# A fused attention and mixture-of-experts kernel: the places of the list fill, of some routing steps, of the first loads and of constant matmuls

## The chip, the cores and the metric

The kernel runs on one core of a Trainium2 chip. The metric is the device time of one execution in microseconds (us); less is better. The median of three executions of the kernel before is 837.98 us.

## The reference

Attention over 8 batches and 8 heads, 576 tokens of 64 values, with a mask by blocks of 64; its output, one row of 512 for each of 4608 tokens, goes through a top-1 mixture of 8 experts. Cut to what matters:

```python
scores = (q @ k.T) / 8                       # for each batch and head, 576 x 576
scores = where(i // 64 >= j // 64, scores, -1e9)
attn = exp(scores - max); attn /= sum(attn) + 1e-9
x = (attn @ v) as rows of 8 * 64             # 4608 x 512
logits = x @ w_gate + modality_bias[modality_id]
e = argmax(logits); gate = softmax(logits)[e]
out = gate * (relu(x @ w1[e]) @ w2[e])       # w1: 512 x 1024, w2: 1024 x 512
```

## The kernel before

Work goes by pairs of heads: 32 pairs, four to a batch. A slot is one pass over the table `ORDER`: it runs the scores, maxima and exponentials of pair `slot` and, one stage later, the transposes, value products and back products of pair `slot - 1`. Slot 0 has its own table, `FIRST`, and the last pass another, `LAST`. Every matmul operand is split into a rounded part and a rest (fp32r), so that three products give nearly full precision: `first_keys`, `first_copies` and `first_queries` do this for pair 0 in three pieces (`PIECES`), `second` for pair 1, `split_qk` on GpSimd for the others, one slot ahead.

The order on each engine, and in SyncE's queue of transfers, is the program's own: within an engine everything waits for what stands ahead of it. Names in the tables: S scores, M maxima (VectorE, `low`, L290), E exponentials (ScalarE), T transposes, C and D their copies and rests (ScalarE and VectorE), X, Y, W the three parts of the value product (`values`, L421), x and y its copies, K the back product (L440, L442), Z the rows (L453); the letter A or B is the head of the pair, t the last 64 tokens of both.

`load` issues the loads of a pair; for pairs 0 and 1 also the mask rows `cm`, four partitions of the tile z, which GpSimd issues. `load_q` issues the queries of the pair two slots on. The rests of the last 64 tokens' probabilities go through the transfer `p<-p4l` (L384), issued at the end of a slot and read in the next slot's value product, part W.

`keep_warm` issues matmuls of constants into a bank that nobody reads at that time; `WARM` says how many ahead of which step.

Routing of a batch (`routing`) is a list of about 28 small steps, most of them on VectorE; `steps` holds those still to come. The places q0 to q7 of `ORDER` take one step each, or two in slots 25 to 30 (from `EARLY`); qp and qv take only the matmul step `counts` and the scan behind it. After the last pair of a batch (place ZB) all steps that are left run at once and the next batch's list begins. Behind batch 5's routing, 22 steps of the expert choice follow in the list (`choose`, through `Later`, kind "pick"). Routing works in the upper half of the bank o0, part X of the value product in its lower half, so X waits for the routing steps ahead of it.

The list of token numbers by expert (`idlist`, in device memory) is first filled with a number that is out of bounds, in eight transfers of 304 KB from one small tile (`prepare_fill`); the scatters of each batch (L579) then write into it. Before, the fill's tile is a part of `btmp`, set by GpSimd as one of batch 0's steps, and the eight transfers are steps too, with empty steps between them.

Of the kernel before, what the change touches and what calls it, by code (L numbers as in the profile page):

```python
# [14 lines left out]
I32 = mybir.dt.int32  # L15
# [9 lines left out]
NPAIR = B * H // 2  # L25
# [40 lines left out]
FIRST += tuple(x for x in ORDER if x[1] == 0 and x not in FIRST and x[0][0] != "q")  # L66

PIECES = ((slice(0, 256), slice(0, 256)), (slice(256, 576), slice(256, 640)), (slice(576, 1280), slice(640, 1280)))
WARM = {(0, "SA3"): 14, (0, "SB01"): 14, (0, "TA0"): 5, (0, "St1"): 8, (0, "TA1"): 16, (0, "TA2"): 12, (1, "TB0"): 6}

EARLY_STEPS = {
    (NPAIR - 2, "SA2"): ("stage", "ids", "cast00"),
# [30 lines left out]
def attention_moe(ctx, tc, qk, vr, bkw, w1, w2, cf, ci, cm, ld, out):  # L103
# [24 lines left out]
    midf = cst.tile([128, 2, B * 5], F32, name="midf")  # L128
    bias = cst.tile([128, B * 5, NE], F32, name="bias")
    btmp = cst.tile([128, B * 5, NE], F32, name="btmp")  # L130
    fill = btmp.rearrange("p a b -> p (a b)").bitcast(I32)[:, 0 : NROW // 128]

    att_stack = ExitStack()
    rt = ctx.enter_context(tc.tile_pool(name="rt", bufs=2, side="right"))
# [25 lines left out]
    xrb = [rt.tile([128, 4, XW], F32, name=f"xr{i}", bufs=1) for i in range(2)]  # L160
    for x in xrb:
        dve.memset(x[:, :, 513:XW], 0.0)
    scatters, placing = [], []
    pairs = [Pair() for _ in range(NPAIR)]
    xrs = {}

    def load(p):
        d = pairs[p]
        d.qk = qkts[p % 3]
        d.q = d.qk[:, 0:1280].rearrange("p (h c) -> p h c", h=2)  # L170
        d.k = d.qk[:, 1280:2432].rearrange("p (h c) -> p h c", h=2)
        d.qt = d.qk[:, 2432:2560]
        d.raw = raws[p % 2]
        d.q2, d.k2, d.pt = q2s[p % 2], k2s[p % 2], pts[p % 2]
        d.s, d.pm, d.copies, d.o, d.ot, d.b = {}, {}, {}, {}, {}, {}
        d.ott = None
        d.rq = att.tile([128, 1280], F32, name="pm", bufs=3) if p == 1 else rawq
        if p == 0:
            for ks, qs in PIECES:
                nc.sync.dma_start(d.raw[:, ks], qk[p][:, 1280:2560][:, ks])  # L180
                nc.sync.dma_start(d.rq[:, qs], qk[p][:, qs])
        elif p == 1:
            for h in range(2):
                ks, qs = halves(h)
                nc.sync.dma_start(d.raw[:, ks], qk[p][:, 1280:2560][:, ks])
                nc.sync.dma_start(d.rq[:, qs], qk[p][:, qs])
        else:
            nc.sync.dma_start(d.raw, qk[p][:, 1280:2560])
        if p < 2:
            pool.dma_start(zs[p][64:68], cm)  # L190

    def load_q(p):
# [504 lines left out]
    def prepare_bias(dst, r):  # L697
# [10 lines left out]
        lambda: pool.tensor_tensor(bias, bias, btmp, ALU.add),  # L708
        lambda: dve.tensor_copy(ranks, iom8),
        lambda: dve.tensor_copy(bases, base8),  # L710
        lambda: pool.memset(fill, int(BIG)),
    ]
    for i in range(IW // 2):
        steps += [lambda i=i: prepare_fill(i)] + [lambda: None] * (0 < i < 6)

    def keep_warm(n):
        for _ in range(n):
# [2 lines left out]
    def run_slot(slot):  # L720
# [7 lines left out]
        for name, stage in LAST if slot == NPAIR else ORDER if slot else FIRST:  # L728
# [13 lines left out]
            if name == "q4" and 0 < slot < NPAIR - 1:  # L742
                load_q(slot + 2)
            if name[0] == "q":
                kinds = (name,) if not name[1].isdigit() else ("",) if name in ("q1", "q4") else ("", "pick")
                for _ in range(2 if EARLY * PPB < slot < NPAIR - 1 and "" in kinds else 1):
                    if slot > 1 and steps and getattr(steps[0], "kind", "") in kinds:
                        steps.pop(0)()
                continue
# [3 lines left out]
            if slot == 0:  # L753
                done.add((name, p))
                if name in first:
                    first[name]()
                    continue
            keep_warm(WARM.get((slot, name), 0))
            emit(name, p)
            if name == "vh":  # L760
                for _ in range(2 if slot % PPB == 0 or slot > EARLY * PPB else 1):
# [11 lines left out]
    with tc.manual_schedule(engines=engines | {ET.SP}):  # L773
        load(0)
        for _ in range(NWARM):
            pe.matmul(bbank, ones, jks[0], start=True, stop=True)
        nc.sync.dma_start(cft[:, 0:128], cf[:, 0:128])
        load(1)
        for i in range(2):
            first_keys(i, dve)  # L780
            first_copies(i)
            if i == 0:
                first_queries(0, dve)
        gather_low(pairs[0], (0,))
        for slot in range(NPAIR + lag):
            run_slot(slot)
# [454 lines left out]
```

## Time and profile before

| | us |
|---|---|
| median of three executions (837.08 to 840.86) | 837.98 |
| the profiled execution | 837.02 |
| its span | 835.2 |
| TensorE busy (matmul) | 815.8 |
| VectorE busy | 444.8 |
| ScalarE busy | 463.5 |
| GpSimd busy | 457.0 |

The profile is of one execution. Busy time is the sum over an engine's instructions; matmuls are pipelined and their ends are modelled, so a TensorE that is busy all the time isn't at its peak. What ends a wait is inferred from semaphore events. By the distance of the L442 matmuls a slot takes 11.4 to 11.7 us from slot 1 on (one 13.5), and some 12.2 us in most of slots 26 to 31; the attention stage ends near 390 us, and then the experts' products follow.

### The profile page before, as it was taken

How to read it: one execution, taken by the hardware profiler on the slowest of the kernel's cores; microseconds unless marked ns; L12 is line 12 of the kernel's file. 1: busy time of each engine (PE TensorE's matmuls, PEld its weight loads, DVE VectorE, ACT ScalarE, POOL GpSimd, SP SyncE). 2: the span in 40 equal slices, each digit the busy share in tenths (PEclk: the TensorE clock that was granted, in tenths of full speed). 3: DMA queues.
4: the chain of work that ended last, by engine and by line, in shares of the span. 5: the costliest groups of instructions: out<-in, count | busy, mean ns of one | idle time of the engine just before them, and what ended most of it. 6: DMA issues, size and time to landing. Idle time of an engine off the chain costs nothing.

```text
span 835.2 us, 15342 instructions
## 1 busy us (share of the span) xinstructions
PE 815.8 (98%) x5151; PEld 730.2 (87%) x5151; DVE 444.8 (53%) x1650; ACT 463.5 (55%) x1387; POOL 457.0 (55%) x306
## 2 busy tenths in 40 slices
PE   7999999999999999999999999999999999999995
PEld 6999999999999999999999888888888888888883
DVE  4888999999999999996631112121222212122110
ACT  5989999999999999996432213121221313132221
POOL 6988889898999989987563431222330302010010
PEclk7999999999999999999999999999999999999998
DMA  8678876768786868666723221131230301110000
GB/s 255 195 221 261 245 228 193 240 194 268 199 255 188 241 205 250 191 162 209 252 65 102 78 79 65 34 102 50 77 127 25 127 26 62 56 38 26 26 34 22
DMA packets 59104, 118.46 MB, mean 142 GB/s; under 512 B 13618, under 2 KB 26738, under 8 KB 59016
## 3 DMA queue, kind: packets, MB, share of 16 engines
q1 hardware_dynamic: 49888, 96.30, 38.3%
q0 software_dynamic: 9136, 21.17, 8.0%
q8 instruction: 42, 0.69, 0.4%
q14 instruction: 38, 0.31, 0.1%
HBM read 77.50 MB, written 22.25 MB: 119 GB/s over the span
## 4 chain that ended last, share of the span: by engine, by line
PE 65%; issue 25%; POOL 4%; DMA 2%; DVE 2%; ACT 0%; POOLq 0%; SPq 0%; DVEq 0%
PE o L421 12%; PE s L1016 8%; PE b L440 6%; PE s L285 5%; PE s L286 5%; PE s L960 4%; PE o L1006 4%; PE o L1029 3%; PE t L344 3%; PE t L349 2%; PE s L277 2%; POOL out L1040 2%; PE b L1029 2%; PE s L1029 2%; POOL xr L917 2%
## 5 line engine op out<-in xcount | busy, mean ns | idle before, releaser
L381 DVE TENSOR_TENSOR ptl<-t,pth 128x512 fp32r<-128x512 f32 (+3 forms) x288 | 140.0, 504 | 17.9 <-ACT pth L374 15.8
L290 DVE TENSOR_SCALAR_CACHE_REDUCE scratch<-s 128x128 bf16<-128x128 f32 (+4 forms) x288 | 132.4, 477 | 13.1 <-PE s L286 10.4
L318 ACT ACTIVATE pm<-s,nm 128x256 f32<-128x256 f32 (+3 forms) x256 | 134.6, 535 | 5.7 <-DVE scratch L290 5.5
L374 ACT CAST pth<-t 128x512 fp32r<-128x512 f32 (+3 forms) x288 | 122.9, 453 | 16.2 <-PE t L344 10.9
L421 PE MATMUL o<-pth,vhl 128*128 128x320 f32 (+3 forms) x384 | 110.2, 306 | 2.0 <-DVE pi L577 0.7
L421 PE MATMUL o<-ptl,vhl 128*128 128x320 f32 (+3 forms) x384 | 110.2, 307 | 0.0
L1040 POOL DMA_INDIRECT out<-scratch,ids_b x17 | 16.8, 986 | 165.4 <-ACT scratch L1039 152.3
L285 PE MATMUL s<-qkt 128*128 128x256 f32 (+3 forms) x256 | 90.4, 366 | 1.4 <-DVE qkt L237 1.3
L214 POOL TENSOR_TENSOR qkt<-rawq,qkt 64x1280 fp32r<-64x1280 f32 x30 | 87.7, 2924 | 2.4
L210 POOL TENSOR_TENSOR z<-raw,qkt 64x1152 fp32r<-64x1152 f32 x30 | 79.7, 2655 | 13.3 <-issue 8.5
L286 PE MATMUL s<-z 68*128 68x256 f32 (+3 forms) x256 | 81.0, 329 | 1.0 <-DMA z<-cm 1.0
L421 PEld LDWEIGHTS o<-pth,vhl 128*128 128x128 f32 x384 | 72.7, 189 | 4.9 <-issue 1.8
L1018 ACT ACTIVATE qkt<-s 128x512 fp32r<-128x512 f32 x28 | 16.7, 598 | 103.9 <-PE s L1016 103.9
L1018 ACT ACTIVATE ptl<-s 128x512 fp32r<-128x512 f32 x28 | 16.8, 598 | 103.0 <-PE s L1016 103.0
L421 PEld LDWEIGHTS o<-ptl,vhl 128*128 128x128 f32 x384 | 72.7, 189 | 1.3
L440 PE MATMUL b<-bk,ot 128*128 128x72 f32 x512 | 64.7, 269 | 0.1
L440 PEld LDWEIGHTS b<-bk,ot 128*128 128x128 f32 x512 | 64.2, 192 | 0.6 <-ACT ott L433 0.6
L318 ACT ACTIVATION_READ_ACCUMULATOR pm<-s,nm 128x1 f32 x256 | 53.3, 208 | 0.0
L285 PEld LDWEIGHTS s<-qkt 128*128 128x128 f32 x256 | 49.7, 194 | 2.4 <-DVE qkt L237 1.8
L286 PEld LDWEIGHTS s<-z 68*128 68x128 f32 x256 | 49.7, 194 | 1.5 <-issue 1.3
L1016 PE MATMUL s<-z,w0hb 128*128 128x512 f32 x128 | 50.6, 395 | 0.0
L1016 PE MATMUL s<-z,w0lb 128*128 128x512 f32 x128 | 50.5, 395 | 0.0
(355 smaller groups left out, 2101.7 us busy)
## 6 DMA issues: line engine op xcount, KB each, us to landing
raw<-qk SPq DMA_DIRECT2D x30, 640.0 KB, 4.2
rawq<-qk SPq DMA_DIRECT2D x30, 640.0 KB, 5.1
raw<-w SPq DMA_DIRECT2D x23, 512.0 KB, 3.5
vrt<-vr SPq DMA_DIRECT2D x32, 320.0 KB, 5.2
k2t<-z SPq DMA_DIRECT2D x64, 144.0 KB, 5.3
xrows<-xr SPq DMA_DIRECT2D x8, 1056.0 KB, 6.6
z<-qkt SPq DMA_DIRECT2D x30, 256.0 KB, 4.8
idlist<-btmp SPq DMA_DIRECT2D x8, 304.0 KB, 6.0
```

What stands on the lines that cost most here:

```text
L210: pool.tensor_tensor(d.k2[0:64], k, d.k[0:64], ALU.subtract)
L214: pool.tensor_tensor(d.q[0:64], q, d.q[0:64], ALU.subtract)
L285: pe.matmul(o, d.q[:, h, qs], d.k[:, h, 0:n], start=True, stop=False)
L286: pe.matmul(o, d.q2[0:68, h, qs], d.k2[0:68, h, 0:n], start=False, stop=True)
L290: dve.tensor_scalar(jks[jturn[0] % 4][:, 0 : s.shape[-1]], s, -SCALE, start, ALU.mult, ALU.min, accum_out=o)
L318: act.activation(d.pm[h][:, CHUNK_OFF[c] : CHUNK_OFF[c] + n], s[:, 256 * i : 256 * i + n], AF.Exp, bias=d.nm[:, h, c : c + 1], scale=SCALE ...
L374: act.copy(dst[0], s)
L381: dve.tensor_tensor(dst[1], s, dst[0], ALU.subtract)
L421: pe.matmul(o, w, r, start=part != "W" and i == 0, stop=part != "Y" and i == len(mm) - 1)
L440: pe.matmul(d.b[h][:, 72 * c : 72 * c + 72], d.ot[h][:, 128 * c : 128 * c + 128], w, start=True, stop=True)
L1016: nc.tensor.matmul(hp, w[:, kc, :], x[kc], start=i == 0, stop=i == len(mm) - 1)
L1029: nc.tensor.matmul(y, x[:, ts], w, start=m == 0 and j == 0, stop=m == 7 and j == 2)
```

## The change

- The fill's source is no longer in `btmp` but in the second row buffer `xrb[1]`; GpSimd sets it once, after the loads of pairs 0 and 1 are issued. The eight fill transfers are no longer steps: two go out in each of slots 1 to 4, ahead of Mt1 and of Ttl.
- In slots 25 to 30 the place q2 takes only steps of the kind "pick", up to two; the other numbered places take up to two, as before.
- Pair 0's queries are issued in ScalarE's queue, its keys as before in SyncE's.
- Pair 0's mask rows come in three transfers, the first with what the first two chunks of head 0 need.
- `WARM`: 40 in place of 14 constant matmuls ahead of the scores SA3 of slot 0, 24 in place of 14 ahead of SB01.

```diff
-WARM = {(0, "SA3"): 14, (0, "SB01"): 14, (0, "TA0"): 5, (0, "St1"): 8, (0, "TA1"): 16, (0, "TA2"): 12, (1, "TB0"): 6}
+WARM = {(0, "SA3"): 40, (0, "SB01"): 24, (0, "TA0"): 5, (0, "St1"): 8, (0, "TA1"): 16, (0, "TA2"): 12, (1, "TB0"): 6}
+
+FILLING = ("Mt1", "Ttl")
...
-    fill = btmp.rearrange("p a b -> p (a b)").bitcast(I32)[:, 0 : NROW // 128]
...
+    fill = xrb[1][:, 0, 0 : NROW // 128].bitcast(I32)
...
-                nc.sync.dma_start(d.rq[:, qs], qk[p][:, qs])
+                act.dma_start(d.rq[:, qs], qk[p][:, qs])
...
-        if p < 2:
+        if p == 0:
+            z, m = (t[:, 0:2048].rearrange("p (a c) -> p a c", a=2) for t in (zs[p][64:68], cm))
+            for cs in (slice(0, 256), slice(256, 1024)):
+                pool.dma_start(z[:, :, cs], m[:, :, cs])
+            pool.dma_start(zs[p][64:68, 2048:2176], cm[:, 2048:2176])
+        elif p == 1:
             pool.dma_start(zs[p][64:68], cm)
...
-        lambda: pool.memset(fill, int(BIG)),
     ]
-    for i in range(IW // 2):
-        steps += [lambda i=i: prepare_fill(i)] + [lambda: None] * (0 < i < 6)
...
-                kinds = (name,) if not name[1].isdigit() else ("",) if name in ("q1", "q4") else ("", "pick")
-                for _ in range(2 if EARLY * PPB < slot < NPAIR - 1 and "" in kinds else 1):
+                fast = EARLY * PPB < slot < NPAIR - 1
+                kinds = (name,) if not name[1].isdigit() else ("",) if name in ("q1", "q4") else ("pick",) if fast and name == "q2" else ("", "pick")
+                for _ in range(2 if fast and name[1].isdigit() else 1):
...
             keep_warm(WARM.get((slot, name), 0))
+            if name in FILLING and 0 < slot <= IW // 4:
+                prepare_fill(2 * slot - 2 + FILLING.index(name))
             emit(name, p)
...
         load(1)
+        pool.memset(fill, int(BIG))
```

What moves is shown at three places. SyncE's queue before, from the key gathers of slot 3 to those of slot 4 (`idlist<-btmp` is the fill, `rawq<-qk` the query load, `p<-p4l` the transfer that the next slot's value product reads, with the program's buffer numbers behind the names):

```order
L203 DMA k2t<-z_102 64x576 x2
L213 DMA z_102<-qkt_109 64x2x512
L689 DMA idlist<-btmp 128x2x304 x2
L194 DMA rawq<-qk 128x1280
L689 DMA idlist<-btmp 128x2x304
L384 DMA p_892<-p4l 64x128
L689 DMA idlist<-btmp 128x2x304
L188 DMA raw_111<-qk 128x1280
L255 DMA vrt<-vr 128x640
L203 DMA k2t<-z_105 64x576 x2
```

The same stretch of the queue after; in slots 1, 2 and 4 it reads alike:

```order
L210 DMA k2t<-z_102 64x576 x2
L220 DMA z_102<-qkt_109 64x2x512
L696 DMA idlist<-xr_115 128x2x304 x2
L201 DMA rawq<-qk 128x1280
L391 DMA p_933<-p4l 64x128
L190 DMA raw_111<-qk 128x1280
L262 DMA vrt<-vr 128x640
```

So the four fills of a slot become two, and none stands between the query load and `p<-p4l` or behind it. At the start of ScalarE's instructions before there is the table load and the first copies:

```order
L231 ACT_TABLE_LOAD
L231 CAST qkt_108<-rawq 128x256
L232 CAST z_102<-rawq 64x256
L231 CAST qkt_108<-rawq 128x384
L232 CAST z_102<-rawq 64x256
```

and after, three transfers stand ahead of them:

```order
L183 DMA rawq<-qk 128x256
L183 DMA rawq<-qk 128x384
L183 DMA rawq<-qk 128x640
L238 ACT_TABLE_LOAD
L238 CAST qkt_108<-rawq 128x256
L239 CAST z_102<-rawq 64x256
```

The copies themselves keep their order. On VectorE, before, this is the end of slot 28 (L94 holds operations of the expert choice, L453 to L456 are the rows of the pair, L477 to L482 the first routing steps of batch 6):

```order
L381 TENSOR_TENSOR p4l<-t,p_5934 64x128
L94 SCALAR_TENSOR_TENSOR b<-oh_a,b 128x8
L94 SCALAR_TENSOR_TENSOR start<-oh_b,b 128x8
L453 TENSOR_TENSOR xr_114<-b,rc 128x4x64
L454 TENSOR_TENSOR gl<-b,rc 128x32
L456 TENSOR_SCALAR xt<-b,ts 128x80
L477 TENSOR_REDUCE o_98<-gl 128x32
L481 TENSOR_REDUCE o_98<-xt 128x8
L482 TENSOR_REDUCE o_98<-xt 128x8
L290 TENSOR_SCALAR scratch,nm<-s 128x384
```

and after, from the rows of the pair on:

```order
L463 TENSOR_SCALAR xt<-b,ts 128x80
L96 TENSOR_REDUCE ix_b<-b 128x1
L96 TENSOR_SCALAR oh_b<-b,ix_b 128x8
L96 TENSOR_SCALAR ei_b<-ix_b 128x1
L96 TENSOR_TENSOR b<-taken,b 128x8
L96 SCALAR_TENSOR_TENSOR dk_a,df_a<-oh_a,b 128x8
L96 CAST di_a<-df_a 128x1
L96 SCALAR_TENSOR_TENSOR dk_r,df_r<-oh_a,b 128x8
L96 CAST di_r<-df_r 128x1
L96 SCALAR_TENSOR_TENSOR dk_b,df_b<-oh_b,b 128x8
L96 CAST di_b<-df_b 128x1
L96 SCALAR_TENSOR_TENSOR b<-oh_a,b 128x8
```

One more of the choice, `start<-oh_b,b`, follows there, and then the same three routing steps; before, these twelve stood spread between the end of slot 27 and the end of slot 28. On TensorE the product with `ones` and `lead` (the step `counts`) stands one slot later for batches 5 and 6, and the routing steps on VectorE behind it too.

## Rows read from the trace of the kernel before

**Rows 1.** Part 2 of the page: the clock granted to TensorE, in tenths of full speed, in 40 slices of 20.9 us each.

```profile
PEclk7999999999999999999999999999999999999998
```

**Rows 2.** Busy time by stretch, 2 us each, from the start of the span. Columns: stretch and its length, then busy us (instructions) of PE, PEld, DVE, ACT and POOL, then granted clock, share of the 16 DMA engines, GB/s.

```profile
6.00:8.00 2.00, 1.35 (x17) 1.13 (x17) 1.36 (x6) 0.48 (x2) 0.00 (x0) 0.99 1.05 375
8.00:10.00 2.00, 1.33 (x3) 1.14 (x4) 0.62 (x2) 1.85 (x8) 1.46 (x2) 0.50 1.04 396
...
12.00:14.00 2.00, 1.87 (x12) 1.76 (x12) 1.10 (x7) 0.67 (x2) 1.96 (x2) 0.50 1.02 297
14.00:16.00 2.00, 2.00 (x8) 1.81 (x7) 0.38 (x3) 1.39 (x5) 1.96 (x2) 0.50 1.08 372
16.00:18.00 2.00, 2.00 (x13) 1.85 (x13) 1.35 (x6) 1.59 (x5) 1.92 (x3) 0.50 0.95 269
18.00:20.00 2.00, 1.78 (x22) 1.47 (x21) 1.13 (x3) 1.75 (x5) 1.92 (x2) 0.95 0.84 285
```

**Rows 3.** What TensorE waited for in the first 20 us: us in total, times, longest.

```profile
PE s L285 <- DVE qkt L237: 1.3, 1, 1.3
PE s L286 <- DMA z<-cm: 1.0, 1, 1.0
```

**Rows 4.** What TensorE waited for from 20 to 500 us: us in total, times, longest.

```profile
PE o L421 <- DMA p<-p4l: 1.8, 1, 1.8
PE o L421 <- DVE pi L577: 0.7, 2, 0.5
...
PE o L421 <- DVE o L482: 0.5, 1, 0.5
```

**Rows 5.** The chain that ended last, in order of time (start us, us, what), within the first 130 us. The L442 rows close the first part of a slot each, so their distance is a slot's length.

```profile
2.26 5.24 DMA rawq<-qk
7.52 0.52 ACT qkt L231
8.06 0.56 DVE qkt L237
...
33.89 0.23 PE b L442 x2
...
45.34 0.23 PE b L442 x2
...
57.23 5.68 DMA p<-p4l
...
70.30 0.23 PE b L442 x2
```

**Rows 6.** Instructions of all engines in order of time in the first 24 us: start us, us, engine, line, operation, out<-in, count, and the idle time before with its releaser. SPq is SyncE's queue of transfers.

```profile
1.32 0.41 SPq L181 DMA_DIRECT2D rawq<-qk  x1
...
1.42 1.26 POOL L190 DMA_DIRECT2D z<-cm  x2 [0.84 <-POOLq L1234]
...
6.39 0.96 PE L718 MATMUL b<-ones 128*128 128x128 bf16 x14
...
9.30 0.73 ACT L231 CAST qkt<-rawq 128x640 fp32r<-128x640 f32 x1 [0.15 <-DMA rawq<-qk]
...
10.33 1.72 PE L718 MATMUL b<-ones 128*128 128x128 bf16 x14
...
10.54 1.49 DVE L237 TENSOR_TENSOR qkt<-rawq,qkt 64x640 fp32r<-64x640 f32 x1
...
12.18 0.45 PE L285 MATMUL s<-qkt 128*128 128x128 f32 x1
...
22.43 0.42 PE L285 MATMUL s<-qkt 128*128 128x384 f32 x1
```

**Rows 7.** SyncE's queue of transfers in the second, third and fourth slot (20 to 60 us), same columns.

```profile
26.73 0.65 SPq L213 DMA_DIRECT2D z<-qkt  x1
...
34.34 0.47 SPq L384 DMA_DIRECT2D p<-p4l  x1
...
54.89 0.92 SPq L689 DMA_DIRECT2D idlist<-btmp  x2
...
56.40 0.47 SPq L689 DMA_DIRECT2D idlist<-btmp  x1
57.23 0.47 SPq L384 DMA_DIRECT2D p<-p4l  x1
```

**Rows 8.** Two rows: the time from issue to landing of the three transfers that read or write the tile z between 23 and 34 us (the two gathers of key rests and the move of query rows at 26.73), and TensorE's first matmul on that tile in the third slot.

```profile
DMA to landing us min/median/max: 6.2/6.3/6.3
...
34.47 0.34 PE L286 MATMUL s<-z 68*128 68x384 f32 x1
```

**Rows 9.** VectorE and TensorE around the end of slot 28 and of slot 30, same columns as rows 6 (L94 is the helper that puts an operation of the expert choice off to a later place).

```profile
341.02 0.15 DVE L94 TENSOR_SCALAR ei_b<-ix_b 128x1 int32<-128x1 f32 x1
...
349.82 0.15 DVE L94 SCALAR_TENSOR_TENSOR b<-oh_a,b 128x8 f32<-128x8 f32 x1
...
351.42 0.21 DVE L482 TENSOR_REDUCE o<-xt 128x8 f32<-128x32 f32 x1
...
351.78 0.36 PE L421 MATMUL o<-pth,vhl 128*128 128x256 f32 x1 [0.48 <-DVE o L482]
...
371.79 0.25 DVE L535 TENSOR_TENSOR_SCAN o<-cf,o 128x40 f32<-128x40 f32 x1 [0.20 <-PE o L526]
...
376.04 0.17 DVE L577 TENSOR_TENSOR pi<-o,cf 128x5 int32<-128x5 f32 x1
```

## The prediction

> **What bounds the kernel now.** I read the clock first. TensorE has its full clock in every slice but the first and the last [rows 1]. Next come the waits: from 20 to 500 us TensorE waits for almost nothing, and the largest entry, 1.8 us, is for one transfer, `p<-p4l` [rows 4]. So behind the first slot the kernel runs at TensorE's pace, and a stall that goes moves everything behind it forward. A change that spares other engines' time, or a transfer's, is worth only what TensorE then no longer waits.
>
> Three places are open. The first slot: 22.43 us pass before TensorE takes up pair 1 [rows 6], the granted clock is 0.50 from 8 to nearly 18 us [rows 2], and the chain there starts with a load of queries [rows 5]. The fourth slot: the fills stand in the transfer queue ahead of `p<-p4l`, and two slots that should take 11.45 us each take 24.96 together [rows 5, 7]. The end of the attention stage: TensorE waits three times, 1.2 us in all, for a routing step on VectorE [rows 4]. They share a bank: routing works in the upper half of o0, the value product writes its lower half, and the product waits for the routing step placed ahead of it.
>
> **The fill.** Before, the fills wait in SyncE's in-order queue until GpSimd has set `btmp`. At 54.89 us three go out within two microseconds with a query load between them, and `p<-p4l`, issued at 57.23, lands 5.68 us later [rows 5, 7]; TensorE waits 1.8 us of this [rows 4]. By slot lengths it is 24.96 - 2 x 11.45 = 2.06 us. After, the source is set at the start, and two fills go out in each of slots 1 to 4 right behind the move of query rows. None stands between the query load and `p<-p4l`. I take -1.9, between the two readings. The other bound is a stall that comes back: slots 1 and 2 get 0.62 MB more each, which at the 0.375 to 0.396 MB per us of [rows 2] is 1.6 us of transfers; `p<-p4l` is issued at 34.34 us in slot 1 [rows 7], some 7 us behind the place of the fills, so I expect most of them to be through. If each of two slots lost 0.8 us, the term would be -0.3. Bounds -2.1 and -0.3. The new place of the memset costs nothing: GpSimd has no busy time from 6 to 8 us [rows 2].
>
> **The first slot.** The chain is: query piece 1 issued at 2.26, landed after 5.24 us, copied by ScalarE 7.52 to 8.04, its rest on VectorE at 8.06, TensorE at 8.66 [rows 5]. The mask rows cost TensorE 1.0 us of waiting at 5 to 6 us [rows 3], but what it then does next waits for that query rest until 8.66 anyway (1.3 us [rows 3]): smaller mask pieces are worth nothing by themselves. They do let the constant matmuls start a microsecond earlier. The queries on ScalarE's queue: an issue took 0.41 us [rows 6] while the landing took 5.24 us [rows 5], so issuing was not what was late, and the engines are already at 375 to 396 GB/s at that time [rows 2]. I take 0 for it; bounds +0.5 (three issues of 0.41 us, 1.2 us in all, now stand ahead of ScalarE's table load) and -0.8 (two places of about 0.4 us earlier).
>
> The Trainium skill, DMA: Bandwidth & Descriptors, section Issuing engines are not separate DMA queues, says that transfers started from several engines run on the same 16 engines and that a second issuer saves only issue time. By it this part would also give at most 0.8 us; an intermixing that helps one piece would have to come out of another.
>
> What is left are the constant matmuls: 40 and 24 in place of 14 and 14. At full clock 14 took 0.96 us, at half 1.72 [rows 6], that is 0.069 and 0.123 us each. The 26 and 10 more are 36 x 0.069 = 2.5 us of work, and fall in TensorE's own gaps: 40 take 2.75 us, from the end of the first scores (6.39, or about 5.4 if the mask comes early) to 8.1 or 9.1, against the next scores' 8.66. The gap from 7.35 to 8.66 closes, and with it the stretch after which the clock fell to 0.50 [rows 2]. What a full clock gives: the two score groups from 8.66 to 10.33 shrink by half, 0.8 us. The next scores need VectorE's rest of query piece 2, which stood behind the maximum of these scores at 10.54 and needs ScalarE's copy, 9.30 + 0.73 = 10.03 [rows 6]: 0.5 us earlier, so TensorE begins at about 11.7 instead of 12.18. From there to 18 us TensorE is busy 1.9 to 2.0 of each 2 us at half clock, but ScalarE has 0.67, 1.39 and 1.59 [rows 2], and it is what binds when the matmuls halve: from 14 to 20 us it has 4.73 of 6 us of work, so about 1.2 us can go. Together 1.7 us.
>
> Not all of this arrives. The chain of GpSimd and transfers for pair 2 is its own: the query rows are issued at 26.73 and land 6.3 us later, at 33.0 [rows 7, 8], while TensorE needs them at 34.47 [rows 8]. A gain beyond 1.47 us would wait there, and fills now load the same engines. I take **-1.1** between 0 and -1.7, nearer to the latter since the gap that precedes the fall is the one that is filled; bounds -1.7 (the 0.8 us of earlier query loads adds nothing to it, since 1.47 us is already less) and +3.9 (below).
>
> The Trainium skill, TensorE: Matmul & The Clock Gate, section What you observe and the callouts behind it, says the half clock is the state without activity and that the moment of the switch differs from run to run of one kernel. No run here shows the second; by it the first-slot term could be 0 in some runs and 1.7 in others.
>
> **The routing places.** In slots 25 to 30 the place q2 takes no more routing steps. By the order the counts of batch 5 and of batch 6 then miss their slot and come one slot later. Seven VectorE operations leave slot 26, and again slot 30 (from the scan to the index, [rows 9], 0.16 to 0.25 us, 1.4 us together). Batch 6's last ones now run after the last attention pair, so the wait of 0.5 us at the value product behind them goes. Against that, twelve operations of the expert choice, from `ix_b` to `start`, stand in one piece at the end of slot 28. Ten of them stood spread over slot 28 (341.02 to 349.82 [rows 9]); one behind the other they take about 0.13 us each, 1.5 us. The logits steps follow, and L482 is what the next value product already waits 0.48 us for (351.42 to 351.78 [rows 9]). So that wait grows to about 2.0 us. If VectorE is the bound there, it does the same work in another order and nothing is lost; if TensorE is, the 1.5 us is lost and some 0.4 us comes back in each of slots 26, 27 and 30. I take +0.2; bounds -1.9 (1.4 + 0.5 gained, burst free) and +1.7.
>
> **Sum.** The profiled execution took 837.02 us (span 835.2), 0.96 below the median of three, 837.98. 837.02 - 1.9 - 1.1 + 0.2 = 834.2; the same distance above it, **835.2**, is my forecast for the median.
>
> **Rivals.** (a) The first slot gives nothing: the landing at 7.52 holds the chain and the clock falls all the same (before, it fell although a group of constant matmuls had just run, and rose again only near 18 us). For it speaks that rows show no load waiting for its issue. 837.98 - 1.9 + 0.2 = 836.3. (b) All bounds come good: -2.1, -1.7, -1.9, so 832.3. For it: VectorE has little idle time at the end, so the burst is free. (c) Slower: the 40 constant matmuls run at half clock, 40 x 0.123 = 4.9 us from 6.39, and the scores begin at 11.3 instead of 8.66, +2.65; the 24 behind them end 2.95 us after the next scores, and the first scores of head B come at 16.1 instead of 12.18, +3.9 in all. With the fill's -1.9 and the routing's +0.2 that is 840.2. It decides at the point where the group outlasts the wait for query piece 1, which at full clock it does by at most 0.45 us and at half clock always. Against it: the stretch before 8 us was granted 0.99 [rows 2]. (d) The fill does not do what it should: its transfers in slots 1 and 2, where loads of pairs 2 and 3 are under way, hold back query rows or `p<-p4l` by as much as they held before. Then 837.98 - 0.3 - 1.1 + 0.2 = 836.8.
>
> **How the numbers follow.** Forecast 0.45 (833.8 to 836.6 by its own bounds), (a) 0.17, (b) 0.20, (c) 0.08, (d) 0.10. All but (b) and (c) lie within 0.5% of 837.98 (833.8 to 842.2), about what a measurement of this kernel can tell from no change; of (b) nearly all lies below, of (c) a third above, with a little for a slip that I haven't named. Faster 0.21, same 0.75, slower 0.04. The range goes from (b)'s 832.3 to 838.4, which leaves out (c) and little else.
>
> **What would show it.** Fill: no wait for `p<-p4l` above 0.5 us, slots 1 to 4 near 11.5 us each. First slot: pair 1's first scores at about 20.8 us and a granted clock of 1.00 from 8 to 18; if the clock is 0.50 there, (a) or (c). Constant matmuls: the scores of query piece 1 at 8.2 to 9.1. Mask: the 1.0 us wait gone, and the scores behind no earlier for it. Routing: a wait of 1.5 to 2 us for L482's successor at the start of slot 29, slots 26 and 30 shorter by some 0.4 us. I am wrong if the first slot gains over 2 us, or if the sum of slots 25 to 31 changes by more than 2 us.

## The result, and the profile after

| | median us | range | executions |
|---|---|---|---|
| kernel before, on the same chip | 839.38 | 836.66 to 840.86 | 10 |
| changed kernel | 843.60 | 840.97 to 846.19 | 10 |

The ratio is 1.0054, 95% interval 1.0035 to 1.0074: slower by about 4.5 us, where 835.2 was forecast. The profiled execution took 842.30 us (span 840.5), 5.28 more than the one of before. In the changed code line numbers are 7 higher from the score lines on (8 among the experts); L449 stands for L442, and L428 for L421.

Where the time went can be read from one row per slot. The L449 row that closes slot 28 stands at 349.77 us, the next at 365.65: slot 29 took 15.88 us. In the kernel before the two rows stood at 349.31 and 361.68: 12.37 us. By such differences the profiled execution lost and gained, in us:

| pair 1 begins | slot 4 | slots 5 to 26 | slot 27 | slot 28 | slot 29 | slots 30, 31 | last part | experts' first product | at 427 to 431 us | rest |
|---|---|---|---|---|---|---|---|---|---|---|
| +1.66 | -2.08 | -0.46 | +0.88 | +0.46 | +3.51 | -0.63 | -0.74 | +0.98 | +1.28 | +0.4 |

**The fill** did what it should. SyncE's queue in slots 1 to 4 (start us, us, what; `idlist<-xr` is the fill), against [rows 7]:

```profile
28.53 1.79 SPq L696 DMA_DIRECT2D idlist<-xr  x2
36.00 0.47 SPq L391 DMA_DIRECT2D p<-p4l  x1
...
53.29 1.35 SPq L696 DMA_DIRECT2D idlist<-xr  x2
58.89 0.47 SPq L391 DMA_DIRECT2D p<-p4l  x1
```

The fills go out 7.5 and 5.6 us ahead of `p<-p4l`, and slot 4 has the length of its neighbours.

**The first slot** got longer. What TensorE waited for in the first 24 us, against [rows 3] (us in total, times, longest):

```profile
PE s L293 <- DMA z<-cm: 2.8, 1, 2.8
```

and its instructions there, against [rows 6]:

```profile
8.07 0.45 PE L293 MATMUL s<-z 68*128 68x128 f32 x1 [2.75 <-DMA z<-cm]
...
8.85 4.31 PE L722 MATMUL b<-ones 128*128 128x128 bf16 x40
12.98 0.48 PE L292 MATMUL s<-qkt 128*128 128x512 f32 x1
...
13.88 1.51 PE L722 MATMUL b<-ones 128*128 128x128 bf16 x24
...
24.09 0.42 PE L292 MATMUL s<-qkt 128*128 128x384 f32 x1
```

The mask rows end the wait at 8.07 instead of 5.97 us. The 40 constant matmuls begin behind them and take 0.108 us each, the 24 after them 0.063: the first group runs at half clock (1.2 GHz) until about 12.9 us, the second at the full 2.4. The scores on query piece 1 begin at 12.98, where they began at 8.66. From there on everything is at full clock, so of these 4.3 us only 1.66 are left at pair 1.

Query piece 1 itself was early: ScalarE copied it at 4.71 us, where it did so at 7.52 before [rows 5]. But VectorE's rest of it stands behind the maxima of the first scores, which wait for the mask rows:

```profile
4.71 0.51 ACT L238 CAST qkt<-rawq 128x384 fp32r<-128x384 f32 x1
...
9.65 0.94 DVE L244 TENSOR_TENSOR qkt<-rawq,qkt 64x384 fp32r<-64x384 f32 x1
```

This rest was done at 10.59 us. At full clock the 40 take 2.41 us (E7 below), so they would have ended near 11.3, already 0.7 us behind it; the half clock adds some 1.7 us more (an estimate from these rows). The row of the granted clock is no help this early:

```profile
8.00:10.00 2.00, 1.93 (x14) 1.87 (x15) 0.91 (x5) 0.24 (x1) 0.58 (x1) 1.00 1.01 339
10.00:12.00 2.00, 2.00 (x22) 2.00 (x20) 0.59 (x1) 1.81 (x6) 1.91 (x3) 1.00 0.67 215
```

It reads 1.00 where the matmuls take 0.108 us, so I go by durations in the first slot. The same holds for the first digit of the 40 slices, 9 now against 7 in [rows 1].

**The routing places.** What TensorE waited for from 20 to 500 us, against [rows 4]:

```profile
PE o L428 <- DVE o L489: 2.4, 1, 2.4
PE o L428 <- DMA p<-p4l: 1.3, 1, 1.3
PE s L968 <- issue: 0.8, 1, 0.8
...
PE o L1014 <- DVE pi L584: 0.7, 1, 0.7
```

The 1.3 us for `p<-p4l` is not the old stall but a new one in slot 27. The 2.4 us stand at the start of slot 29, against [rows 9]:

```profile
351.38 0.16 DVE L96 TENSOR_REDUCE ix_b<-b 128x1 f32<-128x8 f32 x1
...
353.04 0.16 DVE L96 SCALAR_TENSOR_TENSOR start<-oh_b,b 128x8 f32<-128x8 f32 x1
...
353.82 0.21 DVE L489 TENSOR_REDUCE o<-xt 128x8 f32<-128x32 f32 x1
...
354.18 0.55 PE L428 MATMUL o<-pth,vhl 128*128 128x256 f32 x1 [2.43 <-DVE o L489]
```

Twelve operations of the expert choice, 1.8 us, stand ahead of the logits that the value product waits for. Behind that wait the granted clock falls (columns as in [rows 2]):

```profile
352.00:354.00 2.00, 0.00 (x0) 0.00 (x0) 1.76 (x16) 0.38 (x1) 1.92 (x3) 1.00 0.83 225
354.00:356.00 2.00, 1.82 (x8) 1.85 (x9) 1.95 (x11) 1.06 (x5) 2.00 (x1) 0.54 1.00 356
356.00:358.00 2.00, 2.00 (x12) 1.96 (x11) 1.26 (x6) 0.99 (x5) 1.84 (x3) 0.60 1.14 227
358.00:360.00 2.00, 2.00 (x18) 1.87 (x17) 1.79 (x7) 1.45 (x6) 1.70 (x2) 1.00 0.81 296
```

TensorE stood still for over two microseconds, then worked some 3.4 us at half clock ((1 - 0.54) / 0.5 x 2 + (1 - 0.60) / 0.5 x 2 by the rows): 2.4 us of waiting became 3.5 us of slot.

### The profile page after: what moved, and what is told of

Its sections match the earlier page's. It is cut to its first block, busy times and chain, and to the rows that moved or that the text cites. A ratio compares the mean times of both kernels' runs of the same rounds, so it can differ in the third digit from the quotient of the medians.

```text
span 840.5 us, 15430 instructions
## 1 busy us (share of the span) xinstructions
PE 817.6 (97%) x5187; PEld 732.3 (87%) x5187; DVE 444.7 (53%) x1650; ACT 461.2 (55%) x1387; POOL 456.2 (54%) x308
## 4 chain that ended last, share of the span: by engine, by line
PE 63%; issue 26%; POOL 4%; ACT 3%; DVE 2%; DMA 1%; POOLq 0%; SPq 0%; DVEq 0%
PE o L428 12%; PE s L1024 8%; PE b L447 6%; PE s L292 5%; PE s L293 4%; PE s L968 4%; PE o L1014 4%; PE o L1037 3%; PE t L351 3%; PE t L356 2%; POOL out L1048 2%; PE s L284 2%; PE b L1037 2%; PE s L1037 2%; POOL xr L925 2%
## 5 line engine op out<-in xcount | busy, mean ns | idle before, releaser
L428 PE MATMUL o<-pth,vhl 128*128 128x320 f32 (+3 forms) x384 | 110.7, 307 | 2.7 <-DVE o L489 2.4
L428 PE MATMUL o<-ptl,vhl 128*128 128x320 f32 (+3 forms) x384 | 110.8, 309 | 0.0
L428 PEld LDWEIGHTS o<-pth,vhl 128*128 128x128 f32 x384 | 73.2, 191 | 4.6 <-POOL qkt L219 2.6
L428 PEld LDWEIGHTS o<-ptl,vhl 128*128 128x128 f32 x384 | 73.2, 191 | 1.3
L586 POOL DMA_INDIRECT idlist<-idt,pi x40 | 39.7, 993 | 24.9 <-DVE pi L584 9.8
```

The source lines that it names most:

```text
L428: pe.matmul(o, w, r, start=part != "W" and i == 0, stop=part != "Y" and i == len(mm) - 1)
```

## The experiments

Times are medians, with the ratio to the kernel before on the same chip and its 95% interval. The slots' differences are against the profile of before, from the rows that close them. In the expectations of E10, R16, R17 and R18, "slot 1" and "slot 3" are the intervals that begin at those slots' closing rows; the table calls them slot 2 and slot 4.

| run | edit, on top of before | us | ratio |
|---|---|---|---|
| E1 | fill | 834.11 | 0.9952 (0.9934 to 0.9970) |
| E2 | three first-slot edits | 839.51 | 1.0015 (0.9995 to 1.0034) |
| E3 | routing | 840.15 | 1.0034 (1.0009 to 1.0058) |
| E4 | fill, three first-slot edits | 836.95 | 0.9977 (0.9960 to 0.9994) |
| E5 | fill, mask rows in three | 833.76 | 0.9966 (0.9948 to 0.9983) |
| E6 | fill, queries on ScalarE's queue | 834.10 | 0.9960 (0.9942 to 0.9978) |
| E7 | fill, 40 and 24 constant matmuls | 833.40 | 0.9955 (0.9939 to 0.9970) |
| E8 | fill, routing of batch 5 | 838.18 | 1.0010 (0.9991 to 1.0030) |
| E9 | fill, mask rows, queries | 835.38 | 0.9975 (0.9955 to 0.9995) |
| E10 | fill, mask rows, constant matmuls | 832.90 | 0.9943 (0.9927 to 0.9959) |
| E11 | fill, routing of batch 6 | 835.65 | 0.9970 (0.9952 to 0.9988) |
| E12 | E8, choice spread over slot 28 | 836.90 | 0.9989 (0.9968 to 1.0010) |
| R13 | all but the queries | 841.29 | 1.0032 (1.0007 to 1.0056) |

**E1 to E4: the parts by themselves.** Each takes hunks of the change as they stand.

```diff
# E1
+            if name in FILLING and 0 < slot <= IW // 4:
+                prepare_fill(2 * slot - 2 + FILLING.index(name))
# E2
-                nc.sync.dma_start(d.rq[:, qs], qk[p][:, qs])
+                act.dma_start(d.rq[:, qs], qk[p][:, qs])
+            for cs in (slice(0, 256), slice(256, 1024)):
+                pool.dma_start(z[:, :, cs], m[:, :, cs])
+WARM = {(0, "SA3"): 40, (0, "SB01"): 24, ...}
# E3
+                kinds = ... ("pick",) if fast and name == "q2" else ("", "pick")
# E4 is E1 and E2 together
```

> The kernel before with the fill's new place alone. Theory 1 (the parts add, each with what the traces show at its own place): the waits for p<-p4l in slots 3 and 4 go, 2.1 us less than the kernel before, none of it lost later. Theory 2 (the stall was cover: what it held back collides elsewhere, or the routing steps of batch 0, which now begin earlier because the fills no longer stand in the list of steps, cost as much): between -0.5 and +0.5 us.

> The kernel before with the first slot's three edits alone (mask rows in three transfers, queries on ScalarE's queue, 40 and 24 constant matmuls). Theory 1: slower by 1.7 us, as pair 1's first scores came 1.66 us later after the change; the wait for mask rows is again 2.8 us instead of 1.0, the 40 constant matmuls begin near 8.9 us and run at half clock. Theory 2 (the start differs from run to run and the 1.66 us were chance): pair 1's first scores near 22.4 us or before, the time within 0.5 us of the kernel before.

> The kernel before with the routing places alone. Theory 1: the twelve steps of the expert choice in one piece make TensorE wait 2.4 us at the start of slot 29, the granted clock falls to half behind that wait, and the last routing steps make the experts' first product wait: slower by 4 to 5 us, with a stretch at 0.50 near 355 us. Theory 2 (the wait is as long, but the fall of the clock is chance of the run): slower by 2 to 2.5 us. Theory 3 (what was lost there came from the loads' new phase after the other two parts): within 1 us of the kernel before.

> The changed kernel with the routing places as before. Theory 1 (the parts add): fill -2.1 and first slot +1.7, so 0.4 us less than the kernel before, within 0.5 us of it; no stretch at half clock near 355 us. Theory 3 (the loads' phase, not the routing places): 4 to 5 us slower than the kernel before.

E1: slot 4 is 2.08 us shorter, nothing is lost later (-2.0 at the end). Theory 1, but the medians differ by 3.4 us. E2: the wait for mask rows is 3.5 us, the 40 take 4.49 us, pair 1 begins at 26.16: theory 1, the size in the profile larger; the time itself, 0.15% longer, is not clear of noise. E3: the wait of 2.4 us at slot 29 is there, but no fall of the clock: slot 29 longer by 1.95 instead of 3.51. That is theory 2 on the clock; slots 27 and 28 lose 0.68 and 0.47, the experts' first product 0.98. Slot 2 lost 3.47: a landing of 9.15 us for `z<-qkt` made TensorE wait 1.6 us, and behind the wait the granted clock was 0.63 and 0.51 from 36 to 40 us. E4: pair 1 at 24.31, slot 4 -2.08, no wait of 2.4 us, span as before: these two parts add.

**E5 to E7, E9, E10: which first-slot edit.** One or two of the three hunks of E2, with the fill:

```diff
# E5, E9, E10: mask rows
+            for cs in (slice(0, 256), slice(256, 1024)):
+                pool.dma_start(z[:, :, cs], m[:, :, cs])
# E6, E9: queries
+                act.dma_start(d.rq[:, qs], qk[p][:, qs])
# E7, E10: constant matmuls
+WARM = {(0, "SA3"): 40, (0, "SB01"): 24, ...}
```

> The kernel before with the fill's new place and the mask rows in three transfers; queries and constant matmuls as before. The fill alone took 834.1 us. Theory M (small mask pieces land later by themselves): TensorE's wait for z<-cm is 2 to 3.5 us as in the changed kernel. Theory Q (the mask rows are late because the queries, from a queue of their own, take the transfer engines ahead of them): the wait is 1.1 us or less. Time within 1 us of the fill alone in either, since 14 constant matmuls behind the first scores have room before query piece 1.

> The kernel before with the fill's new place and the first pair's queries on ScalarE's queue; the mask rows in one transfer, 14 and 14 constant matmuls. Theory Q: the wait for z<-cm is 2 to 3.5 us. Theory M: 1.1 us or less. Time within 1 us of the fill alone (834.1 us); if the second piece of queries lands earlier and TensorE's scores on it begin before 8.4 us, up to 0.8 us less.

> The kernel before with the fill's new place and 40 and 24 constant matmuls; loads as before. Theory 1 (the group is too long whenever it is not all at full clock): it begins at 5.5 to 6.4 us and takes between 2.75 us (40 x 0.069) and 4.5 us (as in the runs with all three edits); scores on query piece 1 begin up to 10.7 us, pair 1 begins 0.5 to 1.9 us later than with the fill alone, and the time is 834.6 to 836 us. Theory 2 (only the late mask rows make the group late, and full clock comes early): pair 1 begins 0.5 to 1.7 us earlier, 832.4 to 833.6 us.

> The kernel before with the fill's new place, the mask rows in three transfers and the queries on ScalarE's queue; 14 and 14 constant matmuls. Theory Q2 (the two edits on loads together make the mask rows late: neither alone did, with 0 and 1.4 us of wait): the wait for z<-cm is 2.4 to 3.5 us. If the 40 matmuls behind that wait are what makes pair 1 late, pair 1 begins here at 22.0 to 22.7 us in place of 24.1 to 26.2, and the time is that of the fill alone, 834 us. Theory L (the late mask rows alone make pair 1 late): 24 us or later, 835.5 us or more.

> The kernel before with the fill's new place, the mask rows in three transfers and 40 and 24 constant matmuls; the queries on SyncE's queue as before. Theory Q2: no wait for z<-cm, the 40 matmuls begin at 5.7 us or before and end before 8.7, pair 1 begins at 20.4 us, and slot 1 gives 0.6 us of it back to a wait for z<-qkt: 832.5 to 833.8 us, the fastest so far. Theory L2 (the third edit does harm with either of the others): pair 1 at 24 us, 836 us.

| run | wait for mask rows | first group of constant matmuls | pair 1 |
|---|---|---|---|
| E5 mask rows | none | 14 in 1.72 us | 20.54 |
| E6 queries | 1.4 | 14 in 1.16 | 22.49 |
| E7 constant matmuls | 0.6 | 40 in 2.41 | 20.37 |
| E9 mask rows, queries | 3.3 | 14 in 1.72 | 22.55 |
| E10 mask rows, constant matmuls | none | 40 in 2.75 | 21.60 |
| all three (after, E2, E4, R14) | 2.4 to 3.5 | 40 in 3.62 to 4.49 | 24.09 to 26.16 |

Neither M nor Q of E5 and E6 holds alone: only the two edits together make the first scores on mask rows wait until 7.7 us or later (Q2, confirmed by E9). Each edit alone did change the loads: query piece 1 landed 5.1 us after its issue in E1, 3.0 us in E5 and 3.3 in E6. In E5 the scores on it begin at 7.17 us, 1.4 earlier than in E1; in E6 at 8.38, 0.1 earlier, since its rest on VectorE stands behind the maxima of the first scores. In neither does the median show it. Late rows by themselves leave pair 1 where E1 has it, at 22.45 (E9's median is 1.3 us above E1's, with intervals that overlap). E9's rows:

```profile
8.55 0.44 PE L293 MATMUL s<-z 68*128 68x128 f32 x1 [3.30 <-DMA z<-cm]
...
9.33 1.72 PE L722 MATMUL b<-ones 128*128 128x128 bf16 x14
...
22.55 0.42 PE L292 MATMUL s<-qkt 128*128 128x384 f32 x1
```

With 14 there the group ends at 11.05 us, at half clock too; with 40 it ends near 13. And where the rows are early, E7's 40 run at full clock and are harmless (theory 2, pair 1 even earlier than it said):

```profile
6.13 2.41 PE L717 MATMUL b<-ones 128*128 128x128 bf16 x40
...
20.37 0.42 PE L287 MATMUL s<-qkt 128*128 128x384 f32 x1
```

E10 is the fastest kernel of the study, though its pair 1 came at 21.60 us, not at the 20.4 expected. By the ratios E7 lies where E1 does and E10 0.09% below, with intervals that overlap. E4 is E10 with the queries' edit: 0.9977 against 0.9943, with intervals that don't overlap. So beside the other two edits the queries' move costs some 0.3%.

**E8, E11, E12: the routing by halves.**

```diff
# E8
+ ... ("pick",) if fast and slot < 7 * PPB and name == "q2" else ("", "pick")
# E11
+ ... ("pick",) if fast and slot >= 7 * PPB and name == "q2" else ("", "pick")
# E12: E8 and
-                for _ in range(2 if fast and name[1].isdigit() else 1):
+                for _ in range((4 if slot == 7 * PPB and name != "q6" else 2) if fast and name[1].isdigit() else 1):
```

> The kernel before with the fill's new place and the changed routing place in slots 25 to 27 only, so that batch 5's routing alone comes later and the expert choice in one piece; batch 6 as before. Theory 1 (the piece of twelve steps costs what slots 27 to 29 lost): slot 27 longer by 0.7 to 0.9 us, slot 28 by 0.5, slot 29 by 1.9, or by 3.5 where the clock falls behind the 2.4 us wait; 3 to 5 us over the fill alone (834.1 us), and none of the 1 us at the experts' first product. Theory 2 (the loss needs batch 6's change too): within 1 us of the fill alone.

> The kernel before with the fill's new place and the changed routing place in slots 28 to 30 only, so that batch 6's routing alone comes later; batch 5 and the expert choice as before. Theory 1: slots 30 and 31 shorter by 0.6 us each as in the changed kernel, and against that a wait of 0.7 us for the row indices at the experts' first product, about 1 us lost there: within 0.6 us of the fill alone (834.1 us). Theory 2 (half of the change's loss sits here): 835.5 us or more. No wait of 2.4 us at slot 29.

> As the run with batch 5's routing later (838.2 us), but with four steps of the expert choice at each place of slot 28 in place of two, so that they don't stand in one piece at its end. Theory 1 (the piece in front of the value product's bank is the wait): the wait of 2.4 us at slot 29 falls to 1 us or less, no fall of the clock there, slot 29 within 0.6 us of the fill alone; what slots 27 and 28 lose (0.6 and 0.5) stays or goes into waits at other places. Time 834.5 to 836 us. Theory 2 (the wait comes from the batch's late counts, not from the piece): 2.4 us again, 838 us.

E8: slots 27 to 29 lose 0.61, 0.47 and 1.94 us with the clock at 1.00, and the experts' first product nothing: theory 1. E11: slots 30 and 31 give 0.63 us together, not 0.6 each, and against that stand two waits behind them, the first in the last attention pass, with a stretch at half clock behind it, the second at the experts' first product (us in total, times, longest; then the stretch, columns as in [rows 2]):

```profile
PE o L423 <- POOL vhl L264: 1.8, 1, 1.8
PE o L1009 <- DVE pi L579: 1.2, 1, 1.2
```

```profile
388.00:390.00 2.00, 2.00 (x11) 2.00 (x11) 0.00 (x0) 0.00 (x0) 1.08 (x1) 0.50 0.43 127
```

The first costs 2.7 us of that pass (GpSimd's `vhl` was waited for 0.58 us before; why longer here wasn't sought), the second 1.4 us. With 835.65 us, 1.5 above the fill alone, E11 is outside theory 1's 0.6 us and in theory 2's range, but by the ratios its interval overlaps E1's. By the ratios batch 6's part costs 0.18%, batch 5's (E8) 0.58%.

E12: of the twelve steps six are left at the end of slot 28, four ahead of the pair's rows and two behind them, and slot 29 loses 1.0 instead of 1.94 us, though its wait is 1.5 us and not 1 or less. The rest went elsewhere; its waits in the span to 500 us:

```profile
PE o L423 <- DMA p<-p4l: 1.5, 1, 1.5
PE o L423 <- DVE o L484: 1.5, 1, 1.5
...
PE b L442 <- DVE taken L96: 0.8, 1, 0.8
```

Slots 27 and 28 now lose 1.13 and 1.46 us: the choice works in the bank of the gates' product, which waits for it. Theory 1 on the cause, not on the price: 836.9 us, outside the 834.5 to 836 expected.

**R13: the changed kernel without the queries' edit.**

```diff
-                act.dma_start(d.rq[:, qs], qk[p][:, qs])
+                nc.sync.dma_start(d.rq[:, qs], qk[p][:, qs])
```

> The changed kernel with the first pair's queries back on SyncE's queue. Theory Q2 (mask in three and queries on their own queue are harmful only together): no wait for z<-cm, the 40 matmuls at full clock, pair 1 at 20.4 to 21.6 us in place of 24.1; 2 to 3 us less than the changed kernel. The routing part stays: the wait of 2.4 us at slot 29, 3 to 6 us above the run with fill, mask rows and constant matmuls alone (832.9 us). If the 40 and 24 matmuls are to blame whatever the loads do: 24 us and the changed kernel's time.

The 40 take 2.41 us from 5.12 us on, pair 1 begins at 22.10, later than the 20.4 to 21.6 expected, and the wait of 2.4 us at slot 29 stays, with a fall of the clock (slot 29 +3.36). For the mask rows Q2 holds. In the time it isn't shown here: 841.3 us is 2.3 below the changed kernel's median on another chip (by the ratios 0.2%, with intervals that overlap), and 0.9% by ratios above E10.

**R14 to R16: one more profile each** of the changed kernel, of E8 and of E3, with no edit of their own.

> The changed kernel again, one look. Theory C (the fall of the clock at slot 29 comes and goes): the wait of 2.4 us at slot 29 is there, and slot 29 is longer than in the kernel before by 1.9 us (clock 1.00) or by 3.5 us (a stretch at half clock), nothing between. Pair 1 at 24 to 26 us.

> The run with the fill and batch 5's routing later, a second look. The first look had no fall of the clock and a time of 4 us below the kernel's median. Theory C: slot 29 longer by 1.9 or by 3.5 us. If it is 1.9 again and the rest is as in the first look, the median's distance must come from somewhere else.

> The kernel before with the routing places alone, a second look. Theory C: slot 29 longer by 1.9 or by 3.5 us. The 9.15 us landing of the second pair's query rows, which made slot 1 longer by 3.5 us in the first look, gone or again: if it is gone, it was chance of that run.

Slot 29 lost 3.52 (R14), 3.51 (R15) and 1.94 us (R16). With the changed kernel, E3, E8 and R13 that is 1.94 or 1.95 three times and 3.36 to 3.52 four times, with the same 2.4 us wait each time: theory C. E8 and R15 are one kernel (stretches as in [rows 2]), first E8, then R15:

```profile
350.00:352.00 2.00, 0.42 (x4) 0.46 (x5) 1.86 (x12) 0.01 (x1) 1.92 (x3) 1.00 0.81 316
352.00:354.00 2.00, 2.00 (x18) 1.99 (x17) 1.96 (x11) 1.65 (x7) 2.00 (x1) 1.00 1.06 341
```

```profile
350.00:352.00 2.00, 1.00 (x5) 1.03 (x6) 1.93 (x11) 0.58 (x2) 1.92 (x2) 0.80 0.97 388
352.00:354.00 2.00, 2.00 (x9) 1.96 (x9) 1.97 (x12) 1.26 (x6) 2.00 (x2) 0.50 1.03 284
```

R14 shows the same in slot 27, behind a 1.88 us wait for `p<-p4l`: that slot lost 4.65 us.

```profile
330.00:332.00 2.00, 0.33 (x2) 0.33 (x3) 0.58 (x3) 0.00 (x0) 1.92 (x3) 1.00 0.96 328
332.00:334.00 2.00, 2.00 (x10) 1.76 (x10) 0.70 (x2) 1.77 (x9) 2.00 (x1) 0.58 1.00 260
334.00:336.00 2.00, 2.00 (x11) 2.00 (x11) 0.86 (x4) 0.81 (x3) 2.00 (x2) 0.50 0.79 142
336.00:338.00 2.00, 2.00 (x11) 1.90 (x10) 1.18 (x6) 0.84 (x2) 1.84 (x3) 0.50 0.79 262
```

Slot 27 differs as well between E8 and R15: 0.61 us lost in one, 0.02 in the other. In R16 the long landing of E3 in slot 2 was gone, but slot 4, with the old fill, was 4.83 us longer than in the first profile, behind a wait of 3.5 us.

**R17, R18: two more profiles of the kernel before,** no edit.

> The kernel before, a second look. Theory C2 (the stall of slot 3 is followed by a fall of the clock in some executions): if the time is near 836 to 837 us, slot 3 is as in the first profile, within 0.6 us, with clock 1.00; if it is near 840 us or above, slot 3 is longer by 3 to 5 us, with a stretch at 0.50 behind the wait for p<-p4l. Theory D (the two groups come from the first slot, or from the end): slot 3 is the same in both.

> The kernel before, a third look; the same two cases as for the second.

R17 took 837.3 us, slot 4 as in the first profile (-0.16, wait 1.6 us, clock 1.00). R18 took 843.4 us: slot 4 5.72 us longer. Its rows, a wait and the stretches behind it:

```profile
62.19 0.42 PE L421 MATMUL o<-p,vhl 128*128 128x64 f32 x1 [2.79 <-DMA p<-p4l]
```

```profile
60.00:62.00 2.00, 0.00 (x0) 0.00 (x0) 0.19 (x1) 0.00 (x0) 1.23 (x1) 1.00 1.08 402
62.00:64.00 2.00, 1.81 (x6) 1.51 (x7) 0.07 (x1) 0.93 (x5) 1.92 (x2) 0.53 1.06 404
64.00:66.00 2.00, 2.00 (x12) 2.00 (x10) 0.63 (x2) 1.76 (x7) 2.00 (x2) 0.50 1.04 214
```

Behind them the rows read 0.50 until 72 us. Theory C2, by one profile of each kind: the kernel before has the fall of the clock too, in its own stall, in some executions. Beside R13 its 17 times lie in two groups, 7 from 834.9 to 836.9 and 10 from 839.1 to 843.9 us; beside E1 (35), E5 (27) and E9 (35) they spread about as widely, with no such gap in the middle. Slow executions are low in clock: of the 35 beside E1, the 11 above 839 us have a mean granted clock of 0.993 or less, the 11 with 0.995 or more took at most 837.7 us (the mean takes in the first slot too). The 12 of E1, without the stall, lie from 833.0 to 835.8.

## Why the prediction was wrong

**The fill: mechanism right, size too small.** -1.9 was taken, the profiles show 2.08 in every run that has the move. Rival (d) is out: after the change no wait for `p<-p4l` came back in slots 2 to 5. But the step that took 2.06 us from the slot lengths made one execution the price of the stall. In R16 and R18 the same stall cost 6.9 and 7.8 us (2.08 and 4.83, 2.08 and 5.72): the wait was 3.5 and 2.8 us instead of 1.8, and the clock fell behind it. By the medians the move is worth 3.4 us. The profile I read was one of the faster executions.

**The first slot: this term failed, and rival (c) came true by another way in.** The step "smaller mask pieces are worth nothing by themselves" and the 0 for the queries were costed one edit at a time. In time E5 and E6 bear both out (833.76 and 834.10 us against E1's 834.11). The reasons given do not hold: in E5 the scores on query piece 1 do begin earlier, and in E6 the piece lands 2.7 us earlier, 0.9 by its issue and 1.8 by a shorter landing. Together the edits make the first scores on mask rows 1.7 to 2.8 us later than before (E9 and the four profiles with all three edits), which no single row of before could show. What this late start does is near what (c) described: the group outlasts the wait for query piece 1, by some 0.7 us because it starts late and by 1.7 more because it runs at half clock. (c) asked for +3.9, with 4.9 us for the 40; all at half clock they took 4.49 (E2, E4), and the four profiles with all three edits give +1.66 to +3.73. It was held at 0.08 because the stretch before 8 us was granted 0.99, and the late mask rows took just that stretch from under it.

Of the gain of 1.1 us nothing is shown. E7 begins pair 1 at 20.37, near the 20.8 forecast. But the ten profiles with 14 and 14 and the old loads begin it at 20.01 to 22.45 us, E7, E10 and R13 at 20.37 to 22.10. In nine of the ten the clock rows reach back far enough, and pair 1 follows the mean granted clock from 8 to 18 us: 0.50 and 0.51 (pair 1 at 22.43 and 22.45), 0.66 twice (22.01, 21.76), 0.83 four times (20.01 to 21.30), 1.00 in R18 (20.66). The step that failed is "The gap from 7.35 to 8.66 closes, and with it the stretch after which the clock fell". The filled gap doesn't decide: R18 and E5 read 1.00 from 8 to 18 us with 14 and 14 and gaps of 1.6 and 2.7 us, while E10 and R13, with the 40 running up to the next scores, read 0.83. In these two TensorE waited 1.4 and 2.4 us behind the 24, for VectorE's rest of query piece 2: a gap opened there instead.

The Trainium skill, TensorE: Matmul & The Clock Gate, section What you observe, says that the moment of the switch differs from run to run, by half a microsecond either way in a loop of its own. The nine profiles agree that it differs, and by more: in eight of them the clock is back at 1.00 at 11.7 to 18.5 us, and in R18 it doesn't fall in the first slot. The prediction had this as a sentence; it should have been rival (a)'s main argument.

The margin of 1.47 us is not borne out. Slot 2 gave back 0.59 us in E5, which was 1.88 us early, but nothing in R18 and E11, 1.76 and 1.60 early, and 1.73 and 3.47 in E12 and E3, only 1.13 and 0.41 early, at waits for `z<-qkt`.

**The routing places: outside the bounds.** +0.2 between -1.9 and +1.7 was taken. By E4 and the changed kernel it is 0.77% (1.0054 over 0.9977), some 6.5 us; alone on the kernel before it is 0.34%. What was right: the wait of 2.0 us (measured 2.4), and that counts leaving a slot free it (slot 26 gave 0.21, slots 30 and 31 0.6 us). What failed:

- The price if TensorE is the bound, 1.5 us in the text and +1.7 in the bounds, had the wait at its own length (and the text's numbers don't give +1.7: 1.5 less three times 0.4 is 0.3). In four of seven profiles the clock falls behind it, 1.5 us more.
- Slot 27 should have gained 0.4 us and lost 0.88. Before, `p<-p4l`, issued at 325.87 us, landed after 4.1, 0.15 us ahead of its product at 330.12. In the changed kernel the product was ready 0.3 us earlier in its slot, but the transfer landed 1.05 us later: it was issued 0.28 us later in the slot, as in every run with batch 5's routing moved, and took 4.9 us to land (4.0 to 5.5 in those runs). Where it landed after 4.0 (R15), slot 27 lost 0.02 us. I priced the gain without asking what is late next.
- Batch 6's last steps don't vanish from TensorE's path: the experts' first product waits for the row index, 0.97 or 0.98 us lost in four profiles, 1.44 in R16 and E11.
- Of the two waits for the row index in [rows 4] the one in slot 27 (0.25 us) didn't go but moved: TensorE waits as long in slot 28, which loses 0.46 to 0.48 us.

By the sign that the prediction set itself, the sum of slots 25 to 31, it was wrong too: +4.0 us, against the 2 allowed.

**The sum.** By the ratios of E1, E4 and the changed kernel, the fill gave -0.48%, the first slot +0.25% and the routing +0.77%, where -0.23%, -0.13% and +0.02% were forecast. What makes the kernel slower is the routing part. It costs 2.9 us alone on the kernel before (0.8 to 4.9) and 6.5 on top of the rest (4.3 to 8.7, estimated from the two intervals). On the fill alone its halves, 0.58% and 0.18%, give as much as the 0.77%, so it is the small price on the kernel before that stands out. The profiles go with this difference: slots 26 to 32 and the experts' first product together lose 2.5 and 3.1 us in E3 and R16, where the clock fell neither in slot 27 nor in slot 29; 4.2 us in R13 and in the changed kernel's first profile, where it fell in slot 29; 8.0 in R14, where it fell in both. Whether the clock falls there less often on the kernel before, two profiles can't say. Why it falls behind the same wait in one execution and not in the next is not shown either. The 1.28 us at 427 to 431 us (0.8 us of it TensorE waiting for nothing that the profile shows) came in R17 and R18 too, 1.7 and 1.6 us there without any edit, and its cause wasn't sought.

## What to carry to other kernels

A wait of TensorE of some 2 us in mid-kernel should be priced twice, with and without the clock falling behind it, and a profile of one execution shows one of the two: where the times of a kernel spread over more than the stall, profile it again before costing the stall. Edits that touch the same queue or the same transfer engines must be costed together, and filler work behind a wait must be sized for a late start and for the half clock that the wait may bring. A step taken out of a place frees only as much as the next thing is early, and collecting small steps into one piece puts its whole length in front of whoever waits for the last of them.

## What was not expected of the hardware

- The granted clock fell to 0.50 behind waits of 1.6 (E3, slot 2) to 3.5 us (R16) in mid-kernel, for 3.4 to 10.2 us, in some executions of a kernel and not in others: behind the same 2.4 us wait four times of seven, and in the kernel before's own stall in R18 (2.8 us) but not in the first profile (1.8 us) or R17 (1.6 us).
- Query loads on a second queue and mask rows in three small transfers, each harmless alone, together moved the first scores on mask rows to 7.7 to 8.7 us; in the ten profiles with the old loads they begin at 5.0 to 6.3 us. The first transfer of mask rows, 8 KB, then landed 7.0 us after its issue in E2, where the one of 34 KB had taken 4.4 before.
- In the first 12 us, and later in R17, the granted-clock rows of several profiles read 1.00 while a constant matmul of 128 columns took 0.108 to 0.123 us, where it takes 0.060 to 0.069 at full clock (E7 and the first profile); the durations decide there.
